# Deeper rings and new planner numbers in a fused attention and two-layer MoE kernel on one core

## The chip, the cores and the metric

The kernel runs on one core of one Trainium2 chip. Five engines work side by side: TensorE (PE in the profile; PEld is its weight load), VectorE (DVE), ScalarE (ACT), GpSimd (POOL) and SyncE (SP), which here issues nearly all DMAs. Each engine runs its own instructions strictly in order and waits for the others by semaphores. The metric is the device time of one execution in microseconds (us). Before the change it is 602.71 us, the median of three runs (602.31, 602.71 and 603.47).

## The reference

```python
kv  = einsum('bhsd,bhse->bhde', k, v)             # 4 batches, 8 heads, 576 rows, 64 columns
out = einsum('bhsd,bhde->bhse', q, kv)            # attention without a softmax
x   = out / sqrt(mean(out**2, -1) + 1e-6) * g_norm        # 2304 rows x 512
h = x @ w_in                                      # 512 -> 2048
x = (h * tanh(softplus(h))) @ w_out               # 2048 -> 512
h = x @ w2_in                                     # 512 -> 1024
e = exp(h - max(h)); s = h * e / (sum(e) + 1e-9)  # per row
x = ((s - mean(s)) / sqrt(var(s) + 1e-6) * g_ln) @ w2_out # 1024 -> 512
```

The four weight matrices arrive as float64; the device sees each number as two 32-bit words and builds float32 from them.

## The kernel before, in words

Every matrix product is made of three fp16 products of split operands (a number is a high fp16 part plus a low one), so ACT writes the high part of an operand and DVE the low part, always in that order.

**Stages.** The 2304 rows are six blocks of 384 rows (three tiles of 128). First come `kv` of each batch (`kv_pair`, L307) and the attention of each block: `a_xo` (L445, PE) writes a tile into a PSUM bank, `a_xc` (L456, ACT) copies it out for blocks 3 to 5 and frees the bank, then square (L461, ACT), row sums (L465, DVE), the power -1/2 (`a_rho`, L470 and L472, POOL), scaling (`a_xf`, L478, DVE), the split (L487 on ACT, L492 on DVE) and a DMA transpose (`a_xT`, L502) into the operand `xT` of the first layer. All late tiles of `xo` and the `kv` products share one bank. Beside it, 48 weight pieces of 512 KB are loaded and decoded: ACT L561, POOL L566, DVE L571 and L578, then the split L589 on ACT and L596 or L598 on DVE.

The first layer works in units of a block and a quarter of the hidden columns. Blocks 0 to 2 use plain products (`h_mm`, L701); blocks 3 to 5 use a seven-product scheme (`h_prod`, L796) on half blocks, for which `conv_x` and `conv_w` (L732, L738, then ACT L744 and DVE L746 into the tile `ws`) make sums of operands. The tile `ws` lies where the attention's tiles lay, so its first write waits for the last attention transpose. The output product of the first layer is `y_mm` (L870).

The second layer takes pairs of row tiles, p = 0 to 8. `y_split` (L918, L920) makes the split operands of pair p in a region given by `y_form`; `emit_H2` (L975) multiplies; ACT L984 and DVE L997 and L1002 put the products together and find the row maximum. Per tile t then follow `s_max` (L1007, DVE), `s_exp` (L1012, ACT), `s_z` (L1018, DVE), `s_sq` (L1023, ACT), `s_den` and `s_rho` (L1029 to L1039, five POOL instructions on one column; L1038 is the power) and `s_ln` (L1045, ACT). The one-column values of a tile lie in a tile `small`, of which four rotate. The normalised rows of the pair are split again: `s_hi` (L1081, ACT) and `s_lo` (L1087, DVE) write a region that `hl` gives, in three parts a, b and c, and `s_T` (L1092) transposes each part by DMA. For p = 0 the region lies in the dead weights `w1` and in `ws`; for all later pairs it is one region in `g`. `emit_O` (L1111) multiplies, ACT L1122 and L1135 and DVE L1130 put the output together.

**What sets the order.** Nothing is written out in issue order. Every step is a `task` with an engine, a cost in us, the tasks that it waits for, and sometimes a due time. `Plan.order` lists the tasks by simulating these costs and always takes, of the tasks that are ready on an engine, the one with the earliest due time; `Plan.search` repeats this 300 times with due times moved at random and keeps the list that ends PE earliest. The instructions are then emitted in that list's order, and this is the order on every engine. Where the list has PE idle early in the kernel, `keep_warm` (L1613) puts in matmuls on the identity matrix whose results nobody reads (called fillers here); their number is fixed by the list. So a changed cost can change the order on all engines, anywhere.

Of the kernel before, what the change touches and what calls it, by code (L numbers as in the profile page):

```python
# [8 lines left out]
FP32 = mybir.dt.float32  # L9
# [133 lines left out]
def tile_attn_moe_moe2(  # L143
# [14 lines left out]
    B, H, S, D = q.shape  # L158
# [6 lines left out]
    NB = NTOK // BLK  # L165
    NU = NB * 4
    G = 4
# [6 lines left out]
    NI = 3  # L174
# [507 lines left out]
    T = {}  # L682
# [218 lines left out]
    def y_form(p):  # L901
        if p not in yF:
            n = p if p < 7 else p - 7
            x = (w1f, w34["ws"])[n % 2][:, 4096 * (n // 2):4096 * (n // 2) + 14 * HB]
            yF[p] = x.rearrange("p (q a c n) -> p q a c n", q=7, a=2, c=2)
        return yF[p]
# [35 lines left out]
    ph2 = {}  # L942
# [12 lines left out]
    def small(t, name):  # L955
        if (t, "small") not in T:
            T[t, "small"] = ph2["p"].tile([128, len(SMALL)], FP32, tag="small", name="small", bufs=4)
        n = SMALL.index(name)
        T[t, name] = T[t, "small"][:, n:n + 1]
        return T[t, name]  # L960
# [89 lines left out]
    def hl(p, x):  # L1050
        lo, hi = T_OF[x]
        if p:
            t = g_h[:, 1024 * lo:1024 * hi]
        elif x == "b":
            t = w34["ws"][:, 0:3072]
        else:
            t = w1f[:, 0:2048] if x == "a" else w1f[:, 2048:4096]
        return t.rearrange("p (q a f) -> p q a f", a=2, f=512)
# [201 lines left out]
    for c in range(4):  # L1260
        u = (0, c)
# [40 lines left out]
    for b, r in tiles:  # L1302
# [12 lines left out]
        task(("rho", *u), "G", 2.0, a_rho, u, [("ms", *u)] + ring("rho", 3, ("xf", *u)))  # L1315
# [168 lines left out]
    for p in range(NP):  # L1484
        where_ = last_H if p == 6 else [("H", NB - 1, p // 2, 0)] if p < 7 else [("T", 0, x) for x in ("ac" if p == 7 else "b")]
# [26 lines left out]
    for p in range(NP):  # L1512
# [27 lines left out]
        for t in (2 * p + 1, 2 * p):  # L1540
            task(("mx", t), "V", 0.15, s_max, (t,),
# [7 lines left out]
            task(("den", t), "G", 0.5, s_den, (t,), [("ex", t)])  # L1549
            task(("pw", t), "G", 1.1, s_rho, (t,), [("sq2", t), ("den", t)])  # L1550
            task(("ln", t), "A", 1.05, s_ln, (t,), [("pw", t)])
    for p in range(NP):
        gone = lambda x: [("T", p - 1, x)] if p > 1 else dead if p else [("2", "ab".index(x) if x in "ab" else 0, 3)]
# [9 lines left out]
        for x, c in (("a", 1.4), ("b", 2.1), ("c", 1.4)):  # L1563
            buf = [("O", p - 2, i) for i in ORDER] if p > 1 else dead if p else [("Yd", NB - 1, 1)]
            task(("T", p, x), "S", c, s_T, (p, x),
                 [("lo", p, x)] + ([("lo", p, "s")] if x == "b" else []) + buf, 2.6)
# [72 lines left out]
    for key, due in ((("xT", 3, 2), 110.0), (("xT", 4, 2), 125.0), (("xT", 5, 2), 135.0)):  # L1639
        plan.tasks[key][5] = due  # L1640
        plan.hints.add(key)
# [46 lines left out]
```

## Time and profile before

| | |
|---|---|
| median of three runs | 602.71 us |
| the profiled execution | 606.54 us |
| its span, first to last instruction | 604.8 us |
| PE busy | 586.6 us, 97% |
| DVE, ACT, POOL busy | 430.1, 370.1, 134.9 us |
| granted TensorE clock, mean | 0.997 |

The profiled execution took 1.74 us more than its span and 3.83 us more than the median of the runs. PE busy includes the fillers, and a matmul that runs at half clock counts as busy too, so 97% hides time. A timeline row reads: start, duration, engine, line, operation, output from inputs, count, and in brackets how long the engine sat idle before it and what ended that. A row of a table by stage reads: stretch and its length, then busy us of each engine with the number of instructions, the granted clock (1.00 is full speed), the DMA engines' busy share and GB/s.

### The profile page before, as it was taken

To read this page: it belongs to the slowest core of one execution; us is meant where nothing else is said; L and a number is where in the kernel's file an instruction comes from. 1 tells how busy PE (TensorE), PEld (TensorE's weight loads), DVE (VectorE), ACT (ScalarE), POOL (GpSimd) and SP (SyncE) were. 2 spreads that over 40 slices of the span, in tenths; PEclk is the share of its full clock that TensorE was granted. 3 is DMA by queue.
4 is the path that set the end of the run, shared out by engine and by line. 5 is a ranking of instruction groups with operands and counts; after the bars stand their busy time and mean duration, and the time that the engine had idled before them with its cause. 6 is when DMAs were issued, how large, how long until landed. Compare 5 with 4: busy or idle time off the path is not lost.

```text
span 604.8 us, 12057 instructions
## 1 busy us (share of the span) xinstructions
PE 586.6 (97%) x4827; PEld 407.1 (67%) x4827; DVE 430.1 (71%) x722; ACT 370.1 (61%) x633; POOL 134.9 (22%) x180
## 2 busy tenths in 40 slices
PE   8899999997999999999999999999999998999997
PEld 6667665664666667777777877775455665666776
DVE  1698679865877688986658867775657686878751
ACT  3677567565665434554648656655867567898661
POOL 1535341116165000000101100000421133335400
PEclk9999999998999999999999999999999999999999
DMA  8998786999654300011423436205061547757595
GB/s 286 302 270 190 206 196 172 269 242 244 129 126 95 103 1 1 19 60 65 155 90 117 156 104 218 97 17 201 1 123 35 122 81 157 163 119 149 118 209 140
DMA packets 134760, 83.89 MB, mean 139 GB/s; under 512 B 100656, under 2 KB 122160, under 8 KB 134704
## 3 DMA queue, kind: packets, MB, share of 16 engines
q1 hardware_dynamic: 134544, 83.12, 55.1%
q8 instruction: 38, 0.62, 0.4%
q14 instruction: 18, 0.15, 0.1%
q10 hardware_dynamic: 160, 0.00, 0.0%
HBM read 46.67 MB, written 12.06 MB: 97 GB/s over the span
## 4 chain that ended last, share of the span: by engine, by line
PE 71%; DMA 10%; ACT 6%; DVE 5%; POOL 3%; issue 2%; SPq 2%; ACTq 0%; POOLq 0%; DVEq 0%
PE y L870 28%; PE hp L796 14%; PE op L1111 10%; PE h L975 9%; PE hp L701 8%; DMA st<-in_moe_w_in_dram 3%; DMA st<-in_moe_w_out_dram 3%; DMA qraw<-in_q_dram 2%; PE kvp L307 1%; DVE st L571 1%; ACT g L1081 1%; DVE P L578 1%; POOL small L1038 1%; DMA w<-g 1%; POOL small L1039 1%
## 5 line engine op out<-in xcount | busy, mean ns | idle before, releaser
L870 PE MATMUL y<-g,w 128*128 128x384 f16 x1152 | 204.1, 328 | 0.3 <-DVE g L852 0.3
L870 PEld LDWEIGHTS <-w 128*128 128x128 f16 x1152 | 111.4, 98 | 68.6 <-issue 2.0
L566 POOL TENSOR_SCALAR st<-st 128x512 f32<-128x512 f32 x48 | 39.3, 823 | 248.5 <-ACT P L561 246.2
L1111 PEld LDWEIGHTS <-w 128*128 128x128 f16 x756 | 73.9, 98 | 16.3 <-issue 3.6
L701 PEld LDWEIGHTS <-w 128*128 128x128 f16 x576 | 55.4, 98 | 38.6 <-issue 1.4
L1111 PE MATMUL op<-yT,w 128*128 128x256 f16 x567 | 72.2, 273 | 3.0 <-ACT g L1122 2.9
L701 PE MATMUL hp<-xT,w 128*128 128x384 f16 x384 | 66.2, 326 | 0.8 <-DMA xT<-xhl 0.8
L796 PEld LDWEIGHTS <-ws 128*128 128x128 f16 x576 | 48.4, 98 | 3.4
L852 DVE SCALAR_TENSOR_TENSOR g<-m,g 128x768 f16<-128x768 f32 x48 | 45.1, 952 | 7.0 <-ACT g L847 6.8
L561 ACT ACTIVATE P<-st 128x512 f32<-128x512 f32 x48 | 32.1, 672 | 22.4 <-DMA st<-in_moe_w_in_dram 11.4
L571 DVE SCALAR_TENSOR_TENSOR st<-st 128x512 int32<-128x512 int32 x48 | 34.1, 723 | 15.5 <-POOL st L566 15.5
L840 ACT ACTIVATE m<-hp 128x384 f32<-128x384 f32 x48 | 23.0, 486 | 31.8 <-PE hp L701 31.6
L847 ACT ACTIVATE g<-m 128x768 f16<-128x768 f32 x48 | 39.5, 837 | 2.0 <-PE y L870 1.5
L796 PEld LDWEIGHTS <-w 128*128 128x128 f16 x432 | 36.6, 98 | 3.2
L975 PE MATMUL h<-st,w 128*128 128x512 f16 x150 | 35.6, 379 | 1.1 <-DVE small L997 1.1
L835 ACT ACTIVATE m<-m 128x384 f32<-128x384 f32 (+1 forms) x24 | 16.3, 681 | 31.9 <-DVE m L822 31.9
L975 PEld LDWEIGHTS <-w 128*128 128x128 f16 x210 | 20.5, 98 | 22.7 <-issue 1.4
L1029 POOL TENSOR_SCALAR small<-small 128x1 f32<-128x1 f32 x18 | 10.3, 570 | 111.4 <-ACT e L1012 111.0
L578 DVE SCALAR_TENSOR_TENSOR P<-P,st 128x512 int32<-128x512 int32 x48 | 33.2, 710 | 0.3
L701 PE MATMUL hp<-yT,w 128*128 128x384 f16 x192 | 33.0, 326 | 0.3 <-DMA yT<-xhl 0.3
L1111 PE MATMUL op<-ws,w 128*128 128x256 f16 x189 | 30.9, 273 | 0.0
L975 PEld LDWEIGHTS <-ws 128*128 128x128 f16 x168 | 16.4, 98 | 20.6 <-issue 2.6
(161 smaller groups left out, 980.4 us busy)
## 6 DMA issues: line engine op xcount, KB each, us to landing
st<-in_moe_w_in_dram SPq DMA_DIRECT2D x24, 512.0 KB, 5.3
st<-in_moe_w_out_dram SPq DMA_DIRECT2D x24, 512.0 KB, 4.7
yT<-in_k_dram SPq DMA_DIRECT2D x16, 288.0 KB, 5.6
yT<-in_v_dram SPq DMA_DIRECT2D x16, 288.0 KB, 6.4
out_dram<-yT SPq DMA_DIRECT2D x18, 256.0 KB, 2.4
w_far<-F SPq DMA_DIRECT2D x15, 256.0 KB, 2.7
w_far<-st SPq DMA_DIRECT2D x11, 256.0 KB, 2.4
yT<-w_far SPq DMA_DIRECT2D x3, 896.0 KB, 4.7
```

Of the source, the lines that this page charges most:

```text
L561: nc.scalar.activation(out=P, in_=v[:, :, 1], func=ACTF.Copy, scale=2.0 ** -111)
L566: nc.gpsimd.tensor_scalar(out=v[:, :, 1], in0=v[:, :, 1], scalar1=0.0, scalar2=1.0, op0=ALU.mult, op1=ALU.mult)
L571: nc.vector.scalar_tensor_tensor(out=v[:, :, 0], in0=v[:, :, 0], scalar=29, in1=v[:, :, 1], op0=ALU.logical_shift_right, op1=ALU.bitwise_or)
L578: nc.vector.scalar_tensor_tensor(out=P.bitcast(I32), in0=P.bitcast(I32), scalar=3, in1=v[:, :, 0], op0=ALU.logical_shift_left, op1=ALU.bit ...
L701: nc.tensor.matmul(out=h_t[b, grp, i], lhsT=w1[:, f, c, wa], rhs=xT_t[b][:, C * xa + c], start=(c == 0 and m == 0), stop=(c == C - 1 and m ...
L796: nc.tensor.matmul(out=p[:, HT * fs:HT * fs + HT], lhsT=lhsT, rhs=x[:, C * xa + 2 * kx + c, HT * n:HT * n + HT], start=(opens and fs == 0 ...
L840: nc.scalar.activation(out=m_t[b, grp, i // 2][:, i % 2], in_=h_t.pop((b, grp, i)), func=ACTF.Mish, scale=2.0 ** -16)
L847: nc.scalar.activation(out=g_t[b, grp][:, 0, 2 * i:2 * i + 2], in_=m_t[b, grp, i], func=ACTF.Copy, scale=64.0)
L852: nc.vector.scalar_tensor_tensor(out=g_t[b, grp][:, 1, j], in0=m_t.pop((b, grp, i)), scalar=64.0, in1=g_t[b, grp][:, 0, j], op0=ALU.mult, ...
L870: nc.tensor.matmul(out=y_t[cc][:, 0:BLK], lhsT=w2[:, grp * G + ii, wa, cc * 128:(cc + 1) * 128], rhs=g_t[b, grp][:, ga, ii], start=(first ...
L975: nc.tensor.matmul(out=T[p, "2" + bank], lhsT=yF[p][:, x, ya, c], rhs=w3[w][:, c, wa], start=(first and m == 0), stop=(m == 5), skip_group ...
L1111: nc.tensor.matmul(out=T[p, bank][:, 0:HB], lhsT=lnTs[p % 2][:, 8 * x + 4 * la + kk], rhs=w4[kk][:, 7 * HB * wa + HB * w:7 * HB * wa + HB ...
```

## The change

Five things change: the ring of `small` tiles goes from four to eight; `hl` gives two regions in turn (even p in `w1` and `ws`, odd p in `g`), and a write waits for the transposes of the pair two before instead of one before; `y_form` puts pairs 7 and 8 elsewhere, after the H2 products of pairs 3 and 4; six planner costs are raised (POOL's `rho`, `den`, `pw`, the maximum, the scaling `ln`, the transpose's lag); and the due times of three late attention transposes move later.

```diff
-            n = p if p < 7 else p - 7
+            n = p if p < 7 else p - 4
...
-            T[t, "small"] = ph2["p"].tile([128, len(SMALL)], FP32, tag="small", name="small", bufs=4)
+            T[t, "small"] = ph2["p"].tile([128, len(SMALL)], FP32, tag="small", name="small", bufs=8)
...
     def hl(p, x):
         lo, hi = T_OF[x]
-        if p:
+        if p % 2:
             t = g_h[:, 1024 * lo:1024 * hi]
...
-        task(("rho", *u), "G", 2.0, a_rho, u, [("ms", *u)] + ring("rho", 3, ("xf", *u)))
+        task(("rho", *u), "G", 2.4 if b >= NI else 2.0, a_rho, u, [("ms", *u)] + ring("rho", 3, ("xf", *u)))
...
-        where_ = last_H if p == 6 else [("H", NB - 1, p // 2, 0)] if p < 7 else [("T", 0, x) for x in ("ac" if p == 7 else "b")]
+        where_ = last_H if p == 6 else [("H", NB - 1, p // 2, 0)] if p < 7 else [("2", p - 4, 3)]
...
-            task(("den", t), "G", 0.5, s_den, (t,), [("ex", t)])
-            task(("pw", t), "G", 1.1, s_rho, (t,), [("sq2", t), ("den", t)])
-            task(("ln", t), "A", 1.05, s_ln, (t,), [("pw", t)])
+            task(("den", t), "G", 1.0, s_den, (t,), [("ex", t)])
+            task(("pw", t), "G", 2.0, s_rho, (t,), [("sq2", t), ("den", t)])
+            task(("ln", t), "A", 1.24, s_ln, (t,), [("pw", t)])
...
-        gone = lambda x: [("T", p - 1, x)] if p > 1 else dead if p else [("2", "ab".index(x) if x in "ab" else 0, 3)]
+        gone = lambda x: [("T", p - 2, x)] if p > 1 else dead if p else [("2", "ab".index(x) if x in "ab" else 0, 3)]
...
-                 [("lo", p, x)] + ([("lo", p, "s")] if x == "b" else []) + buf, 2.6)
+                 [("lo", p, x)] + ([("lo", p, "s")] if x == "b" else []) + buf, 3.3)
...
-    for key, due in ((("xT", 3, 2), 110.0), (("xT", 4, 2), 125.0), (("xT", 5, 2), 135.0)):
+    for key, due in ((("xT", 3, 2), 140.0), (("xT", 4, 2), 160.0), (("xT", 5, 2), 170.0)):
```

The order changes from the first weight pieces to the end. Three places follow.

**ACT, the attention of block 3.** L456 copies a tile of `xo` out of the shared bank, L487 is the split that needs POOL's power, L561 starts the decoding of a weight piece. Before:

```order
L456 ACTIVATE xf<-xo 128x512
L461 ACTIVATE sq<-xf 128x512
L561 ACTIVATE P<-st 128x512 x2
L456 ACTIVATE xf<-xo 128x512
L461 ACTIVATE sq<-xf 128x512
L487 ACTIVATE xhl<-xf 128x512
L890 ACTIVATE yT<-y_1252 128x384
L419 ACTIVATE qhl<-qraw 128x512
L456 ACTIVATE xf<-xo 128x512
```

and now:

```order
L456 ACTIVATE xf<-xo 128x512
L561 ACTIVATE P<-st 128x512
L461 ACTIVATE sq<-xf 128x512
L890 ACTIVATE yT<-y_1652 128x384
L456 ACTIVATE xf<-xo 128x512
L419 ACTIVATE qhl<-qraw 128x512
L461 ACTIVATE sq<-xf 128x512
L890 ACTIVATE yT<-y_1739 128x384
L561 ACTIVATE P<-st 128x512
L419 ACTIVATE qhl<-qraw 128x512
L840 ACTIVATE m<-hp 128x384
L487 ACTIVATE xhl<-xf 128x512
```

The first split L487 has moved behind the second copy by seven rows; the third copy now stands seven rows further on. On PE the second and third `xo` of the block had one group of 12 matmuls of 384 columns between them and now have six.

**ACT, the second layer, from pair 2 to pair 4.** The outputs of L1081 are the regions of `hl`; `w_69` is `w1`. Before, the last write of pair 2 and, three rows on in this list, the first of pair 3 both go to `g`:

```order
L1081 ACTIVATE g<-Q 128x2x512
L1023 ACTIVATE e,small<-w_69,small 128x1024
L1135 ACTIVATE yT<-op 128x256
L1081 ACTIVATE g<-w_69 128x512
L1012 ACTIVATE e,small<-Q,small 128x1024
L984 ACTIVATE P<-h_5582 128x512
L1045 ACTIVATE w_69<-w_69,small 128x1024
```

and now, from the last write of pair 3 (to `g`) to the first of pair 4:

```order
L1081 ACTIVATE g<-w_69 128x2x512
L1023 ACTIVATE e,small<-Q,small 128x1024
L1081 ACTIVATE ws<-Q 128x512
L1122 ACTIVATE g<-op 128x256
L1012 ACTIVATE e,small<-Q,small 128x1024
L1122 ACTIVATE g<-op 128x256
L1045 ACTIVATE Q<-Q,small 128x1024
```

The write that follows a pair's last write to `g` now goes to `ws`, which the pair two earlier used, and waits for that pair's transpose.

**DVE, the last attention tiles and the first conversion.** L492 ends a tile's attention on DVE, L738 and L746 are the sums and the low halves of `ws` for the first seven-product unit, L822 belongs to that unit itself. Before:

```order
L492 TENSOR_TENSOR xhl<-xf,xhl 128x512
L852 SCALAR_TENSOR_TENSOR g<-m,g 128x768
L571 SCALAR_TENSOR_TENSOR st<-st 128x512
L770 TENSOR_TENSOR xs<-st,xs 128x768
L852 SCALAR_TENSOR_TENSOR g<-m,g 128x768
L770 TENSOR_TENSOR xs<-st,xs 128x768
L578 SCALAR_TENSOR_TENSOR P<-P,st 128x512
L732 TENSOR_TENSOR st<-w_69 128x1024 x2
L738 TENSOR_TENSOR st<-st 128x2x256 x4
L746 TENSOR_TENSOR ws<-st,ws 128x1024 x2
```

and now:

```order
L492 TENSOR_TENSOR xhl<-xf,xhl 128x512
L746 TENSOR_TENSOR ws<-st,ws 128x1024 x2
L852 SCALAR_TENSOR_TENSOR g<-m,g 128x768
L894 SCALAR_TENSOR_TENSOR yT<-y_2557,yT 128x384
L732 TENSOR_TENSOR st<-w_69 128x1024 x2
L894 SCALAR_TENSOR_TENSOR yT<-y_2590,yT 128x384
L822 TENSOR_TENSOR m<-hp,st 128x2x192
```

The last attention tile (L492) now stands directly ahead of the low halves of `ws`, and the first L822 five rows behind them; before, two more conversions stood between those halves and the first L822.

## Rows read from the trace of the kernel before

**Rows 1.** Busy time by stage: PE, PEld, DVE, ACT, POOL, clock, DMA.

```profile
140.00:160.00 20.00, 17.26 (x176) 10.61 (x176) 13.09 (x20) 12.66 (x25) 9.16 (x9) 0.91 0.88 187
160.00:480.00 320.00, 320.00 (x2512) 223.43 (x2510) 235.14 (x391) 185.50 (x314) 39.83 (x54) 1.00 0.32 90
480.00:580.00 100.00, 94.05 (x670) 65.30 (x668) 73.47 (x140) 78.19 (x124) 39.12 (x63) 1.00 0.67 136
```

**Rows 2.** Timeline of PE around 140 to 146 us, the rows with idle time.

```profile
140.40 0.83 PE L445 MATMUL xo<-kvr,qT 128*128 128x128 f16 x12 [0.81 <-ACT xf L456]
...
145.52 0.92 PE L307 MATMUL kvp<-yT 96*64 96x64 f32 x24 [2.34 <-ACT xf L456]
```

**Rows 3.** Chain that ended last (start, us, what): the same group of 12, twice.

```profile
146.44 3.73 PE y L870 x12
...
173.29 1.95 PE y L870 x12
```

**Rows 4.** One microsecond by stage: PE busy, clock, DMA.

```profile
147.00:148.00 1.00, 1.00 (x5) 0.50 0.76 103
```

**Rows 5.** Timeline of ACT and DVE around 140 us.

```profile
137.89 0.67 ACT L561 ACTIVATE P<-st 128x512 f32<-128x512 f32 x1 [1.77 <-DMA st<-in_moe_w_out_dram]
...
141.84 1.13 DVE L478 SCALAR_TENSOR_TENSOR xf<-xf,rho 128x512 f32<-128x512 f32 x1 [1.82 <-POOL rho L472]
...
143.00 0.63 ACT L487 ACTIVATE xhl<-xf 128x512 f16<-128x512 f32 x1 [2.00 <-DVE xf L478]
```

**Rows 6.** Timeline of PE from 480 to 580 us, the rows with idle time.

```profile
485.70 1.46 PE L975 MATMUL h<-st,w 128*128 128x512 f16 x6 [1.12 <-DVE small L997]
...
502.56 1.46 PE L975 MATMUL h<-st,ws 128*128 128x512 f16 x6 [1.04 <-ACT P L984]
...
513.69 1.14 PE L1111 MATMUL op<-yT,w 128*128 128x256 f16 x9 [1.54 <-ACT g L1122]
...
558.82 1.46 PE L975 MATMUL h<-st,ws 128*128 128x512 f16 x6 [0.68 <-ACT P L984]
...
576.06 1.14 PE L1111 MATMUL op<-yT,w 128*128 128x256 f16 x9 [1.40 <-ACT g L1122]
```

**Rows 7.** Timeline of DVE and ACT: what these PE waits stood behind.

```profile
484.94 0.69 DVE L997 CUSTOM_DVE_ANT_0 Q<-h,yT 128x512 f32<-128x512 f32 x1 [4.84 <-ACT Q L1045]
...
500.27 0.63 ACT L1081 ACTIVATE g<-w 128x512 f16<-128x512 f32 x1 [3.38 <-DMA w<-g]
...
574.50 1.24 ACT L1045 ACTIVATE Q<-Q,small 128x1024 f32<-128x1024 f32 x1 [2.04 <-POOL small L1039]
```

**Rows 8.** Timeline of POOL's power, twice, and of DVE beside the second.

```profile
443.77 0.55 POOL L1038 TENSOR_TENSOR small<-small,nhalf 128x1 f32<-128x1 f32 x1
...
552.70 3.40 POOL L1038 TENSOR_TENSOR small<-small,nhalf 128x1 f32<-128x1 f32 x1
...
554.47 1.22 DVE L1018 SCALAR_TENSOR_TENSOR Q<-Q,e 128x1024 f32<-128x1024 f32 x1
```

**Rows 9.** Timeline of the longest run of fillers, and DVE at its end.

```profile
45.73 7.37 PE L1613 MATMUL hp<-ident 128*128 128x256 f16 x66
...
52.54 0.74 DVE L598 SCALAR_TENSOR_TENSOR w<-P,gs,w 128x512 f16<-128x512 f32 x1
```

**Rows 10.** Timeline from the last attention product to the first product with `ws`.

```profile
184.22 0.83 PE L445 MATMUL xo<-kvr,qT 128*128 128x128 f16 x12
...
195.22 1.24 SPq L502 DMA_TRANSPOSE yT<-xhl  x1
...
208.99 1.06 ACT L744 ACTIVATE ws<-st 128x1024 f16<-128x1024 f32 x1 [1.95 <-DVE st L738]
...
211.91 1.23 DVE L746 TENSOR_TENSOR ws<-st,ws 128x1024 f16<-128x1024 f32 x1 [0.61 <-ACT ws L744]
...
235.62 1.15 PE L796 MATMUL hp<-xs,ws 128*128 128x192 f16 x12
```

**Rows 11.** The line L502, the attention's transposes: from issue to landing.

```profile
DMA to landing us min/median/max: 3.1/3.4/6.1
```

More of the change, by code (lines that the diff above doesn't have):

```diff
@@ L1540, in tile_attn_moe_moe2 @@
         for t in (2 * p + 1, 2 * p):
-            task(("mx", t), "V", 0.15, s_max, (t,),
+            task(("mx", t), "V", 0.2, s_max, (t,),
                  [("h21", p), ("h22", p)] if t % 2 else [("h11", p), ("h12", p)])
```

## The prediction

> **What bounds the kernel now.** I read the table by stage first, then the timeline of PE for the rows with idle time, then for each of them the engine that it names, back to what that engine stood behind. From 160 to 480 us PE is busy all 320.00 us at full clock [rows 1]: nothing that happens there can be gained, only lost. PE waits in three other places.
>
> The first is 140 to 151 us. PE waits 0.81 and 2.34 us for ACT's copy L456, which frees the shared bank [rows 2]; the group of 12 matmuls behind the second wait takes 3.73 us where it takes 1.95 later [rows 3]. There the granted clock is 0.50, the lower level of 1.2 GHz [rows 4]; what PE had done before was to stand still for 2.34 us. So the place costs 0.81 + 2.34 + (3.73 - 1.95 = 1.78) = 4.93 us. Where ACT was: it waited 1.77 us for a weight piece that had not landed; then its split L487 waited 2.00 us for DVE, which waited 1.82 us for POOL's power, and the copy that PE needed stood behind that split [rows 5], as the order shows. It is a queue in the wrong order, not too much work: ACT is busy 12.66 of 20 us here [rows 1].
>
> The second is the second layer, 480 to 580 us: PE 94.05 of 100 us, DVE 73.47, ACT 78.19 [rows 1]. Five waits carry it: 1.12, 1.04, 1.54, 0.68 and 1.40 us, sum 5.78 [rows 6]. They have three causes. The 1.12 us: DVE's L997, which empties the PSUM bank, waited 4.84 us for ACT's L1045 [rows 7]. L997 also writes the first value of a new `small` tile, and with four of them in turn the new tile takes the place of one whose last reader is that L1045. The 1.04 us: ACT's L1081 waited 3.38 us for the DMA transpose of the pair before, which still read the one region in `g` [rows 7], and the copy L984 that PE needed stood behind it. The other three (1.54 + 0.68 + 1.40 = 3.62 us): ACT stood at L1045, waiting for POOL's last value (2.04 us for the last of the three [rows 7]), with the copy that PE needed behind. POOL's power takes 0.55 us at one time and 3.40 us at another [rows 8].
>
> The third is the start, where the fillers hide the waits. The longest run, 66 matmuls, takes 7.37 us [rows 9].
>
> **The change part by part.** I sum against the profiled execution, 606.54 us, and carry the sum to the median of the runs, 602.71, at the end.
>
> *The ring of eight.* No instruction is added; the tile that L997 takes is now one of eight tiles earlier, whose L1045 ran four pairs before. The wait of 4.84 us goes, and with it PE's 1.12. What is late next for that L997 is its product, which had been ready. Term: -1.12.
>
> *Two regions in turn.* Same instructions, other addresses. The transposes of the pair two before were issued a whole pair of PE work earlier, so the 3.38 us of ACT go and PE's 1.04 with them. The regions for even p are dead weights: in the new order ACT's writes to them wait for a DMA or DVE, and none of the later pairs' for PE. Term: -1.04.
>
> *Pairs 7 and 8 split later.* The splits and sums move from before the H2 product of pair 4 to among pairs 4 and 5. Their eight copies and the DVE work now fall at 480 us and after, where ACT and DVE have some 22 and 27 us free in 100 [rows 1]. Queued behind them are the copies L984 for PE. Between nothing and one wait like those seen (1.54 us [rows 6]); I take 0.5, within the term for new waits.
>
> *POOL's costs.* The planner had 1.1 us for the three instructions behind the square; now 2.0. So it puts more ACT work between the square L1023 and the L1045 of the same tile. Counted in the order, five of the 18 tiles had nothing or a single copy between the two, and one has now; but a chain with a power of 3.40 us in it [rows 8] is not covered by 2.0. At best all 3.62 go, at worst none. I take half, as the new order covers a short chain but not a long one: -1.81.
>
> Here a rule of the Trainium skill bears on the rows. The long power ran from 552.70 to 556.10, and inside that time DVE ran, among others, L1018, a product of two tiles, to 555.69 [rows 8]. The page "SBUF — State Buffer", section "🔬 SBUF: two separate sides", says that GpSimd and VectorE share one pair of ports as an exclusive lock: an instruction of DVE with two SBUF inputs holds it to its end and the other engine is blocked. The trace agrees: the power ends 0.41 us behind that product. By this rule POOL's time is not a cost that can be planned; it depends on which DVE work falls beside it, and a reordered list draws anew. The term would be 0 and the sum below -5.6 instead of -7.4.
>
> *Late attention.* In the new order of PE the second and third attention products of block 3 have six groups of 12 matmuls between them instead of one, 6 x 1.95 = 11.7 us [rows 3], and ACT's third copy has both first splits well ahead of it. The wait of 2.34 us and the half clock behind it should go; between the first and second product only one group is left, so a wait like the 0.81 may stay in part. Term: -(4.93 - 0.5) = -4.43.
>
> *The start.* The list has 14 fillers fewer behind the first products of the first layer. At 7.37 / 66 = 0.112 us each that is 1.6 us if nothing else is late. But at the end of the long run DVE had only just begun the low half of a weight piece that the next products need, at 52.54 against the run's end at 53.10 [rows 9], and DVE's list up to there is nearly the same. Between 0 and -1.6; I take -0.5.
>
> *New waits.* A list that has not run has waits of its own in 60 to 260 us, where the order is new. Bounds: none, and another place like the one at 140 us, 4.93. The nearest row is a single wait of 0.81 [rows 2]; I take two of them, with the half microsecond of pairs 7 and 8 among them: +1.5.
>
> Sum: -1.12 - 1.04 - 1.81 - 4.43 - 0.5 + 1.5 = -7.4 us, or 599.1 for an execution like the profiled one. That one was 3.83 us slower than the median, so some of its long chains are its own; I let the median keep 6/7 of the gain: 602.71 - 6.3 = 596.4 us.
>
> **The rivals.**
>
> *The waits only move* (no gain in the second layer beyond the two rings, a wait like that of 140 us elsewhere). For it: POOL's chains keep their length, as in [rows 8], and the order of all engines is drawn anew. Against it: two of the causes are removed and not moved. Price: 1.12 + 1.04 + 4.43 gained, 4.93 lost again, -1.66, of which 6/7: 601.3. The port rule above leads here.
>
> *All waits go.* -1.12 - 1.04 - 3.62 - 4.93 - 1.6 = -12.3, no new ones, of which 6/7: 592.2. For it: neither ACT nor DVE is full in any stage [rows 1]. Against it: POOL's 3.40 us.
>
> *Slower: the first conversion comes too late.* The tile `ws` may not be written before the last attention transpose, and that tile's product has moved later: in the order only 12 groups of full matmuls and two groups of half size now lie between the last L445 and the first product with `ws`: 12 x 1.95 [rows 3] and twice 1.15 at most [rows 10], some 25 us, where there were 235.62 - 184.22 = 51.4. The chain that must fit: from the product to the transpose's issue 11.0 us (184.22 to 195.22), 3.4 us to land in the median and 6.1 at most [rows 11], and the two ACT and two DVE halves from 208.99 to 213.14, 4.2 us [rows 10]: about 19 us. It fits with 6 us to spare. DVE's list now has these halves five rows ahead of the unit's first sum, so if DVE and ACT run 6 us behind on the attention, PE stops. At 12 us behind it costs 6 us and some 1.8 of half clock behind the stop [rows 3], and the three further conversions follow on DVE at the same distance, each able to add: -7.4 + 7.8 + some 2 more = +2.4, about 605. Below 6 us behind it costs nothing. Nothing in the rows shows such a backlog, but 26 of the 32 us to spare are gone.
>
> *It doesn't do what it says* (the region or ring not the cause): then the two waits of 1.12 and 1.04 stay: -5.2, of which 6/7, 598.2; inside the forecast's own range.
>
> **How the numbers follow.** Forecast, 593 to 600 with 596.4: chance 0.52. Waits only move, 600 to 603: 0.18. All waits go, below 593: 0.15. Slower, above 603: 0.15. A run of this kernel can tell 0.2% (1.2 us) from no change: faster means below 601.5, within means 601.5 to 603.9. Of the second case about half lies below 601.5. So faster 0.52 + 0.15 + 0.08 = 0.75, same 0.11, slower 0.14. The range leaves out the lowest part of the third case and most of the last: 590 to 603.5.
>
> **What would show it.** Ring: no row of L997 waiting for L1045 or POOL by several us. Regions: no L1081 that waits over 1 us for `w<-g`. Late attention: no PE wait on L456 over 1 us between 130 and 200 us, and the clock at 1.00 in every stage up to 480. POOL: L1045's waits for L1039 in 480 to 580 us fewer than before, PE's waits on L1122 and L984 under 2.5 us in sum. Start: the first seven-product group not later than before. Wrong would be: PE idle before the first product with `ws`, a clock of 0.5 anywhere from 60 to 480 us, or PE busy in 480 to 580 us at 94 of 100 again.

## The result and the profile after

The changed kernel takes 596.14 us, the median of four runs (595.62 to 598.38), against 603.09 us for the kernel before beside it (602.31 to 604.91): ratio 0.9888, 95% interval 0.9853 to 0.9922. It is faster by more than the 0.2% that can be told apart. In a later comparison on one chip the same two kernels gave 594.79 against 604.05 us, ratio 0.9839 (0.9815 to 0.9863). So the gain is 7 to 9 us; 596.4 had been forecast.

The profiled execution of the changed kernel took 596.47 us. Its span is 594.7 us where before had 604.8, and its mean clock is 1.000. That difference of 10.1 us is larger than that of the medians, since the profiled execution of before holds the stretch at half clock [rows 4]. Of the 68 executions of before that were timed beside the experiments, 13 have a mean granted clock of 0.997 or less; they took 606.63 us in the mean, and the 55 at 0.999 or 1.000 took 603.59. The median of before, 603.09, is near the second of these.

The table by stage of the changed kernel, with the columns of [rows 1]:

```profile
140.00:160.00 20.00, 19.39 (x191) 12.57 (x190) 10.49 (x17) 10.48 (x20) 5.41 (x6) 1.00 0.84 216
160.00:480.00 320.00, 319.35 (x2575) 222.53 (x2574) 238.23 (x396) 190.13 (x321) 47.88 (x61) 1.00 0.34 91
480.00:580.00 100.00, 98.71 (x746) 72.84 (x745) 76.99 (x144) 78.05 (x124) 35.73 (x58) 1.00 0.79 156
```

In the last row PE is busy 98.71 of the 100 us, where it was busy 94.05, and the granted clock is 1.00 in all three rows. The timeline of the changed kernel's PE has five waits over 0.3 us behind 50 us:

```profile
53.11 1.80 PE L701 MATMUL hp<-xT,w 128*128 128x384 f16 x10 [0.47 <-DVE w L598]
58.82 3.41 PE L701 MATMUL hp<-xT,w 128*128 128x384 f16 x20 [0.72 <-DMA xT<-xhl]
146.91 0.92 PE L307 MATMUL kvp<-yT 96*64 96x64 f32 x24 [0.61 <-DMA yT<-in_v_dram]
177.85 0.92 PE L307 MATMUL kvp<-yT 96*64 96x64 f32 x24 [0.65 <-DMA yT<-in_v_dram]
566.17 1.14 PE L1111 MATMUL op<-yT,w 128*128 128x256 f16 x9 [1.29 <-ACT g L1122]
```

No wait on L456 is left [rows 2], and of the five in the second layer [rows 6] one. The two at 147 and 178 us are new: PE waits there for the loads of `v`, not for ACT.

The 10.1 us are gained as follows. Up to the first layer-1 product of block 1 (start 58.59 before, 58.82 now) nothing is gained. From there to the first H2 product it takes 349.13 instead of 355.72 us: 2.43 us of waits and 1.78 us of half clock are gone, one output group of 12 matmuls (1.95 us) has moved behind that product, and 0.4 us is in no row. From the first H2 product to the end it takes 186.74 instead of 190.46 us, with that group more: 5.94 us of waits have become 1.29, and 1.0 us is in no row.

### The profile page after: what moved, and what is told of

It is laid out like the page before. It is cut to its first block, busy times and chain, and to the rows that moved or that the text cites. A ratio compares the mean times of both kernels' runs of the same rounds, so it can differ in the third digit from the quotient of the medians.

```text
span 594.7 us, 12020 instructions
## 1 busy us (share of the span) xinstructions
PE 583.9 (98%) x4813; PEld 407.4 (69%) x4813; DVE 431.5 (73%) x722; ACT 370.3 (62%) x633; POOL 136.8 (23%) x180
## 4 chain that ended last, share of the span: by engine, by line
PE 86%; DMA 8%; DVE 2%; issue 1%; SPq 1%; ACT 1%; POOL 1%; POOLq 0%; DVEq 0%
PE y L870 30%; PE hp L796 14%; PE h L975 14%; PE hp L701 13%; PE op L1111 13%; DMA st<-in_moe_w_in_dram 3%; DMA yT<-in_v_dram 3%; DMA st<-in_moe_w_out_dram 2%; PE xo L445 1%; PE kvp L307 1%; DMA xT<-xhl 1%; DVE P L578 0%; POOL small L1039 0%; DVE st L571 0%; SPq L262 0%
## 5 line engine op out<-in xcount | busy, mean ns | idle before, releaser
L566 POOL TENSOR_SCALAR st<-st 128x512 f32<-128x512 f32 x48 | 37.4, 785 | 233.7 <-ACT P L561 232.1
L852 DVE SCALAR_TENSOR_TENSOR g<-m,g 128x768 f16<-128x768 f32 x48 | 46.9, 987 | 10.4 <-ACT g L847 10.3
L561 ACT ACTIVATE P<-st 128x512 f32<-128x512 f32 x48 | 32.0, 673 | 26.2 <-DMA st<-in_moe_w_in_dram 13.2
L1029 POOL TENSOR_SCALAR small<-small 128x1 f32<-128x1 f32 x18 | 15.5, 860 | 97.1 <-ACT e L1012 96.6
```

The source lines that it names most:

```text
L561: nc.scalar.activation(out=P, in_=v[:, :, 1], func=ACTF.Copy, scale=2.0 ** -111)
L566: nc.gpsimd.tensor_scalar(out=v[:, :, 1], in0=v[:, :, 1], scalar1=0.0, scalar2=1.0, op0=ALU.mult, op1=ALU.mult)
L852: nc.vector.scalar_tensor_tensor(out=g_t[b, grp][:, 1, j], in0=m_t.pop((b, grp, i)), scalar=64.0, in1=g_t[b, grp][:, 0, j], op0=ALU.mult, ...
```

## The experiments

Each ratio is the one on record, with its 95% interval; it is not always exactly the quotient of the two medians beside it (599.89 / 604.05 is 0.9931, on record is 0.9912). "Second layer" below means PE's waits from 470 us on; the five of [rows 6] sum to 5.78 us before (5.94 with one of 0.16), and after they come to 1.29. The words of an edit such as "the six costs" mean those lines of the diff above, and all else is the kernel before unless said. The list of before is drawn again by nearly every edit; where an edit leaves the list, or a part of it, word for word as it was, I say so, since only there does the edit act alone.

### The ring alone

```diff
-            T[t, "small"] = ph2["p"].tile([128, len(SMALL)], FP32, tag="small", name="small", bufs=4)
+            T[t, "small"] = ph2["p"].tile([128, len(SMALL)], FP32, tag="small", name="small", bufs=8)
```

> The kernel before with eight small tiles instead of four; the list of instructions is the same on every engine, only the addresses of the one-column values differ. Theory of places (each edit carries its own term): DVE's L997 no longer waits for ACT's L1045, PE's 1.12 us at that place goes, 6/7 of it in the median: ratio 0.9984 (0.9978 to 0.999). Theory of the redrawn list (the gain of the change comes from the new order as a whole): a ring alone does nothing, ratio 1.000, since the same L1045 holds the copy that PE needs a moment later.

Measured: 601.81 against 604.58 us, ratio 0.9948 (0.9931 to 0.9965), 2.8 us, more than either theory had. The waits of the second layer that are left, on PE:

```profile
501.45 1.45 PE L975 MATMUL h<-st,ws 128*128 128x512 f16 x6 [0.48 <-ACT P L984]
503.06 2.75 PE L975 MATMUL h<-st,ws 128*128 128x512 f16 x12 [0.16 <-ACT yT L984]
512.58 1.14 PE L1111 MATMUL op<-yT,w 128*128 128x256 f16 x9 [1.54 <-ACT g L1122]
574.09 1.14 PE L1111 MATMUL op<-yT,w 128*128 128x256 f16 x9 [1.39 <-ACT g L1122]
```

With the list unchanged, the 1.12 us went, and with it half of the 1.04 (I had put that down to the region) and the 0.68 us (put down to POOL). DVE's wait of 4.84 us is gone; that its earlier work behind that point is what shortened the other two is argued and not shown.

### Ring and regions

```diff
-            n = p if p < 7 else p - 7
+            n = p if p < 7 else p - 4
...
-        where_ = last_H if p == 6 else [("H", NB - 1, p // 2, 0)] if p < 7 else [("T", 0, x) for x in ("ac" if p == 7 else "b")]
+        where_ = last_H if p == 6 else [("H", NB - 1, p // 2, 0)] if p < 7 else [("2", p - 4, 3)]
...
-            T[t, "small"] = ph2["p"].tile([128, len(SMALL)], FP32, tag="small", name="small", bufs=4)
+            T[t, "small"] = ph2["p"].tile([128, len(SMALL)], FP32, tag="small", name="small", bufs=8)
...
-        if p:
+        if p % 2:
...
-        gone = lambda x: [("T", p - 1, x)] if p > 1 else dead if p else [("2", "ab".index(x) if x in "ab" else 0, 3)]
+        gone = lambda x: [("T", p - 2, x)] if p > 1 else dead if p else [("2", "ab".index(x) if x in "ab" else 0, 3)]
```

> The kernel before with eight small tiles, two regions in turn and pairs 7 and 8 split later; old costs and old due times. The dependences of pairs 7 and 8 reach back through the list, so the order is new everywhere. Theory of places: the waits of 1.12 and 1.04 us go, the ones on POOL stay, and a wait of some us on L456 in the attention of block 3 is there as long as the split L487 stands ahead of the third copy; -1.9 us, ratio 0.997 (0.994 to 0.999). Theory of the redrawn list: a time anywhere between 596 and 606 us, with the attention's wait present or not regardless of the due times.

Measured: 599.09 against 604.58 us, ratio 0.9915 (0.9891 to 0.9938), 5.5 us. Pairs 7 and 8 are split later here too, so "ring and regions" below holds that part as well. The regions can't be run without the ring: with four `small` tiles a step of that list waits for one that stands behind it, and the kernel would never end. The second layer has one wait left:

```profile
571.18 1.14 PE L1111 MATMUL op<-yT,w 128*128 128x256 f16 x9 [1.29 <-ACT g L1122]
```

So ring and regions take PE's waits in the second layer from 5.94 to 1.29 us with the old costs, the one of 1.54 behind POOL [rows 6] among them. Both theories had these stay or move.

### The due times alone

```diff
-    for key, due in ((("xT", 3, 2), 110.0), (("xT", 4, 2), 125.0), (("xT", 5, 2), 135.0)):
+    for key, due in ((("xT", 3, 2), 140.0), (("xT", 4, 2), 160.0), (("xT", 5, 2), 170.0)):
```

> The kernel before with only the three due times moved (140, 160, 170). The list is new up to the first layer's end; in the second layer it is the same as before. The third copy L456 of block 3 still stands right behind the first split L487, and only one group of 12 matmuls lies between the second and third xo. Theory of places, as I had put it: the due times carry the 4.43 us, ratio 0.994 (0.992 to 0.996), and the second layer keeps PE's five waits. Rival: the due times only move the block later as a whole, the split still stands ahead of the copy, so a wait of 1 to 3 us on L456 stays at the new place and the gain is under 2 us, ratio 0.997 to 1.001.

Measured: 604.09 against 604.58 us, ratio 0.9982 (0.9956 to 1.0008): nothing that can be told, as the rival had it. The block comes 20 us later, and its waits with it:

```profile
146.11 0.92 PE L307 MATMUL kvp<-yT 96*64 96x64 f32 x24 [0.75 <-DMA yT<-in_v_dram]
160.50 0.83 PE L445 MATMUL xo<-kvr,qT 128*128 128x128 f16 x12 [0.99 <-ACT xf L456]
168.66 0.92 PE L307 MATMUL kvp<-yT 96*64 96x64 f32 x24 [0.81 <-ACT xf L456]
175.64 0.92 PE L307 MATMUL kvp<-yT 96*64 96x64 f32 x24 [1.11 <-DMA yT<-in_v_dram]
```

3.66 us in four pieces, where before had 3.15 in two [rows 2]. The second layer, whose list is that of before, keeps 5.36 us of its 5.94.

### The six costs alone

```diff
-        task(("rho", *u), "G", 2.0, a_rho, u, [("ms", *u)] + ring("rho", 3, ("xf", *u)))
+        task(("rho", *u), "G", 2.4 if b >= NI else 2.0, a_rho, u, [("ms", *u)] + ring("rho", 3, ("xf", *u)))
...
-            task(("mx", t), "V", 0.15, s_max, (t,),
+            task(("mx", t), "V", 0.2, s_max, (t,),
...
-            task(("den", t), "G", 0.5, s_den, (t,), [("ex", t)])
-            task(("pw", t), "G", 1.1, s_rho, (t,), [("sq2", t), ("den", t)])
-            task(("ln", t), "A", 1.05, s_ln, (t,), [("pw", t)])
+            task(("den", t), "G", 1.0, s_den, (t,), [("ex", t)])
+            task(("pw", t), "G", 2.0, s_rho, (t,), [("sq2", t), ("den", t)])
+            task(("ln", t), "A", 1.24, s_ln, (t,), [("pw", t)])
...
-                 [("lo", p, x)] + ([("lo", p, "s")] if x == "b" else []) + buf, 2.6)
+                 [("lo", p, x)] + ([("lo", p, "s")] if x == "b" else []) + buf, 3.3)
```

> The kernel before with only the six costs raised. The list is new from the first weight pieces to the end. Theory of places: PE's waits behind POOL's power in the second layer (3.62 us) halve, those on the ring and on the region stay, and the attention's wait may stay: -1.55 us in the median, ratio 0.9974 (0.995 to 0.999). Port theory (POOL's long powers come from DVE's instructions beside them and cannot be planned): no gain in 480 to 580 us, ratio 1.000. Redrawn list: the attention of block 3 changes too (its first split now stands behind the second copy by nine rows), and the gain, if any, is there and not in the second layer.

Measured: 595.85 against 604.58 us, ratio 0.9856 (0.9833 to 0.9880), 8.7 us: as much as the whole change, without ring, regions or due times. Neither the places nor the port theory allowed for it, and the theory of the redrawn list had no gain in the second layer, where 5.94 us of waits have become 1.13. All of PE's waits over 0.15 us behind 50 us:

```profile
129.41 0.83 PE L445 MATMUL xo<-kvr,qT 128*128 128x128 f16 x12 [0.68 <-ACT xf L456]
478.53 1.46 PE L975 MATMUL h<-st,w 128*128 128x512 f16 x6 [0.57 <-DVE small L997]
583.62 1.16 PE L1111 MATMUL op<-yT,w 128*128 128x256 f16 x9 [0.56 <-DMA w<-g]
```

In the attention, this list has five groups of 12 matmuls on PE between the third product of block 3 and the `kv` product that needs its copy, where before has one.

### Three of the costs alone

```diff
-            task(("den", t), "G", 0.5, s_den, (t,), [("ex", t)])
-            task(("pw", t), "G", 1.1, s_rho, (t,), [("sq2", t), ("den", t)])
-            task(("ln", t), "A", 1.05, s_ln, (t,), [("pw", t)])
+            task(("den", t), "G", 1.0, s_den, (t,), [("ex", t)])
+            task(("pw", t), "G", 2.0, s_rho, (t,), [("sq2", t), ("den", t)])
+            task(("ln", t), "A", 1.24, s_ln, (t,), [("pw", t)])
```

> The kernel before with three of the six costs raised: den 1.0, pw 2.0, ln 1.24 (POOL's two steps and ACT's scaling in the second layer). The list is the same as before up to the second layer, so the attention keeps its waits of 0.81 and 2.34 us on L456 and the half clock in some executions; only the order of the second layer is new. Theory of the costs (their order covers POOL's chain, and by that also the ring and the region): PE's five waits, 5.78 us, shrink to 1.5 or less in sum, -4 us in the median, ratio 0.9935 (0.991 to 0.996). My prediction's term: half of 3.62, and the ring's 1.12 and the region's 1.04 stay, ratio 0.9974. Port theory: the waits on POOL come back at other tiles, ratio 1.000.

Measured: 602.66 against 603.31 us, ratio 0.9993 (0.9971 to 1.0016): no gain that can be told, though my own term (0.9974) lies within that interval. Only the second layer's list is new here, and the ring's wait on PE has grown:

```profile
483.45 1.46 PE L975 MATMUL h<-st,w 128*128 128x512 f16 x6 [1.99 <-DVE small L997]
500.28 1.46 PE L975 MATMUL h<-st,ws 128*128 128x512 f16 x6 [1.02 <-ACT P L984]
501.90 2.75 PE L975 MATMUL h<-st,ws 128*128 128x512 f16 x12 [0.16 <-ACT yT L984]
511.52 1.14 PE L1111 MATMUL op<-yT,w 128*128 128x256 f16 x9 [1.63 <-ACT g L1122]
```

The waits of 0.68 and 1.40 us at the end are gone, the 1.54 behind POOL is still there (1.63); the sum is 4.80 us. So it isn't the true costs of POOL's steps by themselves that empty the second layer; which of the other three does, with them, was not tried. The clock may hide a part of what these costs gave: five of the 12 executions have a mean clock of 0.998 or less, against two of 29 of before beside them, and the others took 602.2 us in the mean against 603.2. Why the lower clock was more frequent, with the attention's list of before, is open. This run tells one thing more: its attention has the list of before word for word, at a mean clock of 0.999 in the profiled execution, and its waits there are 1.04, 0.20 and 0.55 us, not 0.81 and 2.34. So an execution without the half clock can pay some 1.8 us at that place, and not 4.93; the 3.0 us that the executions of before with the lower mean clock took more fit that (4.93 - 3.0 = 1.9).

### All but the due times

```diff
-    for key, due in ((("xT", 3, 2), 140.0), (("xT", 4, 2), 160.0), (("xT", 5, 2), 170.0)):
+    for key, due in ((("xT", 3, 2), 110.0), (("xT", 4, 2), 125.0), (("xT", 5, 2), 135.0)):
```

(Against the changed kernel.)

> The kernel after with the old due times: costs, ring and regions. Up to the second layer the list is that of the kernel with the six costs alone, with one wait of about 0.7 us in the attention; in the second layer ring and regions are in. Theory of the costs: nothing is left for ring and regions but the two waits of 0.57 and 0.56 us that the costs alone left; ratio 0.9850 (0.983 to 0.988), at or up to 1 us below the costs alone and 1 to 3 us below the full change. My prediction's terms: without the due times 4.43 x 6/7 = 3.8 us of the gain are missing, ratio 0.995.

Measured: 595.80 against 603.31 us, ratio 0.9877 (0.9845 to 0.9909), not to be told from the full change. My terms had 3.8 us of the gain missing here, and they are not missing. The attention has no wait over 0.15 us, the second layer one of 1.28.

### Another seed, no number changed

```diff
-        rng = random.Random(1)
+        rng = random.Random(3)
```

> The kernel before with another seed of the search (3 for 1) and no number changed: the list differs from the first weight pieces to the end of the attention, and is the same behind it. In it the third copy L456 of block 3 stands behind two splits L487 instead of one, with one group of 12 matmuls between second and third xo. Theory of the queue (the split ahead of the copy makes the wait): a wait of 1 to 4 us on L456 as before, ratio 1.000 (0.997 to 1.003). Theory of the redrawn list (any new draw is as likely to gain): the wait is gone or much smaller, ratio 0.993 to 0.997. In both the second layer keeps its 5.8 us.

Measured: 605.96 against 603.31 us, ratio 1.0049 (1.0028 to 1.0071), slower than either theory said. A new draw alone costs 2.7 us here. `Plan.search` moves only the due times of tasks that its list has before 160 us, so the second layer's list is that of before and keeps its waits. The wait on L456 isn't there; two on the loads of `v` are:

```profile
123.37 1.45 PE L307 MATMUL kvp<-yT 96*64 96x64 f32 x24 [2.15 <-DMA yT<-in_v_dram]
153.57 0.92 PE L307 MATMUL kvp<-yT 96*64 96x64 f32 x24 [1.07 <-DMA yT<-in_v_dram]
```

The two splits ahead of the copy, on which I had expected the wait, cost nothing with three groups of PE between the third product and the `kv` product. Behind the first of these waits the clock falls (0.81 in 125 to 130 us), and 11 of the 12 executions have a mean clock of 0.998 or less.

### The six costs with another seed

Beside the six cost lines:

```diff
...
-        rng = random.Random(1)
+        rng = random.Random(2)
```

> The kernel before with the six costs raised and another seed (2 for 1): the second layer's list is that of the six costs with the first seed, the first layer's and the attention's is another draw; there two splits stand ahead of the third copy L456 of block 3, with five groups of 12 matmuls between the second and third xo. Theory of the costs: the second layer's gain of 4 to 5 us is there whatever the draw, ratio 0.985 to 0.992, and the attention costs under 1.5 us more or less than in the first draw. Theory of the redrawn list: the gain of the six costs was one lucky draw; ratio 0.993 to 1.000.

Measured: 601.03 against 603.31 us, ratio 0.9955 (0.9929 to 0.9980). The second layer, whose list the seed leaves as it was, has 0.56 and 0.65 us of waits, so its gain doesn't hang on what is drawn ahead of it. The time does: a wait of 2.54 us for a load of `v` at 26 us with half clock behind it, and in the attention three more:

```profile
128.57 0.83 PE L445 MATMUL xo<-kvr,qT 128*128 128x128 f16 x12 [0.56 <-DVE kvr L324]
132.69 0.83 PE L445 MATMUL xo<-kvr,qT 128*128 128x128 f16 x12 [1.34 <-ACT xf L456]
153.49 0.92 PE L307 MATMUL kvp<-yT 96*64 96x64 f32 x24 [1.79 <-DMA yT<-in_v_dram]
```

With one set of costs, two draws differ by 5 to 6 us (595.85 and 601.03 us; ratios 0.9856 and 0.9955, from two comparisons). Each theory was half right.

### One `kv` product moved by hand

```diff
     order = plan.search(300, 8.0)
+    at_key = {k: n for n, (_, k) in enumerate(order)}
+    a, l, c, y = (at_key[k] for k in (("kv", 3, 0), ("ld", 3, 2), ("kv", 3, 1), ("Y", 1, 1, 2)))
...
+    order[a:c] = [(order[a][0], order[n][1]) if n == y else order[n] for n in range(a + 1, c) if n != l] + [
+        (order[y][0] + 1.0, order[a][1]), (order[l][0] + 1.0, order[l][1])]
```

> The list of before with one move by hand and no new search: the first kv product behind the third late xo (and the load of the batch that waits for it) goes behind the next group of 12 matmuls; all else stands as before. Theory of the queue (PE meets the copy L456 too early): PE's wait of 2.34 us shrinks to 0.4 or less, the stretch at half clock behind it is gone, and the executions with a mean granted clock under 0.999 get rare; median -2 us, ratio 0.9965 (0.994 to 0.998). Rival: the loads of v come later and the next kv products wait for them instead, 1 to 2 us; ratio 0.999 to 1.001. In both the second layer keeps its 5.8 us.

Measured: 607.07 against 604.05 us, ratio 1.0037 (1.0019 to 1.0055): slower, beyond what the rival had. PE in the attention of block 3:

```profile
141.10 0.83 PE L445 MATMUL xo<-kvr,qT 128*128 128x128 f16 x12 [1.23 <-ACT xf L456]
...
146.32 1.62 PE L307 MATMUL kvp<-yT 96*64 96x64 f32 x48 [0.50 <-ACT xf L456]
147.88 2.12 PE L870 MATMUL y<-g,w 128*128 128x384 f16 x12
153.29 1.14 PE L307 MATMUL kvp<-yT 96*64 96x64 f32 x24 [3.29 <-DMA yT<-in_v_dram]
```

The wait on L456 shrank from 2.34 to 0.50 us, as the theory of the queue has it, and 3.29 us came back two `kv` products on. SyncE shows why; the loads of the fourth batch in this kernel:

```profile
147.28 0.33 SPq L262 DMA_DIRECT2D yT<-in_k_dram  x1
147.66 0.46 SPq L262 DMA_DIRECT2D yT<-in_v_dram  x1
```

Two buffers serve these loads in turn, so a load may not be issued before the `kv` product two before it has read its buffer; that one began at 146.32, and the product that needs the load ran at 153.29, 7.0 us later. Before, the same two began at 145.52 [rows 2] and 153.00, 7.5 us apart and without a wait: two groups lay between them, one at half clock (3.73 us [rows 3]), and now a single one. So the place has two limits, the copy and the load, and a move by one group trades one for the other.

### All but the costs

```diff
-        task(("rho", *u), "G", 2.4 if b >= NI else 2.0, a_rho, u, [("ms", *u)] + ring("rho", 3, ("xf", *u)))
+        task(("rho", *u), "G", 2.0, a_rho, u, [("ms", *u)] + ring("rho", 3, ("xf", *u)))
...
-            task(("pw", t), "G", 2.0, s_rho, (t,), [("sq2", t), ("den", t)])
+            task(("pw", t), "G", 1.1, s_rho, (t,), [("sq2", t), ("den", t)])
...
```

(Against the changed kernel; all six lines go back.)

> The kernel after with the six old costs: ring, regions and late due times. Theory of substitutes (ring with regions, or the new costs, either alone empties the second layer's waits): second layer as after, about 1.3 us of waits; the attention's list is another draw, with three groups of 12 matmuls between the third xo and the kv product behind it, so under 2 us of waits there; ratio 0.990 (0.987 to 0.994). My prediction's terms: 1.81 x 6/7 = 1.55 us of the gain are missing, all in 480 to 580 us, where POOL's waits are back at half of 3.62 or more; ratio 0.9915. Theory of the costs as the sole cause: nothing left, 0.997 or above.

Measured: 599.89 against 604.05 us, ratio 0.9912 (0.9886 to 0.9938), the figure of my terms, and not for their reason. The second layer has 1.00 and 0.18 us of waits. The 1.00 stands behind POOL: ACT waits 2.48 us for POOL's last value, and the copy L984 that PE needs comes at the end of the work that ACT then does without a break.

```profile
549.00 1.24 ACT L1045 ACTIVATE Q<-Q,small 128x1024 f32<-128x1024 f32 x1 [2.48 <-POOL small L1039]
...
551.36 0.58 ACT L984 ACTIVATE F<-h 128x512 f32<-128x512 f32 x1
...
551.99 2.75 PE L975 MATMUL h<-P,w 128*128 128x512 f16 x12 [1.00 <-ACT F L984]
```

Yet this is no more than the changed kernel's 1.29. Of the 3.3 us between the two profiled executions, 1.15 lie ahead of the first layer-1 product of block 1, 1.8 between that and the first H2 product (with the group counted that has moved), and 0.4 behind it. The longest waits ahead of the second layer:

```profile
53.62 1.80 PE L701 MATMUL hp<-xT,w 128*128 128x384 f16 x10 [1.49 <-DVE w L598]
59.97 2.27 PE L701 MATMUL hp<-xT,w 128*128 128x384 f16 x13 [0.53 <-DMA xT<-xhl]
169.22 0.83 PE L445 MATMUL xo<-kvr,qT 128*128 128x128 f16 x12 [1.93 <-ACT xf L456]
```

### The changed kernel again, and costs with the ring

The first is the changed kernel itself. The second is the kernel before with the six cost lines and

```diff
-            T[t, "small"] = ph2["p"].tile([128, len(SMALL)], FP32, tag="small", name="small", bufs=4)
+            T[t, "small"] = ph2["p"].tile([128, len(SMALL)], FP32, tag="small", name="small", bufs=8)
```

> The changed kernel once more, beside the candidate below and on one chip with it: ratio 0.9885 to before (0.986 to 0.991).

> The kernel before with the six costs and eight small tiles, and neither regions nor due times: the list is that of the six costs alone, word for word, and only the ring is added. Theory of substitutes: of the two waits of 0.57 us (DVE's L997 behind POOL in the ring) and 0.56 us that the costs alone left, the first goes; ratio 0.985 (0.982 to 0.988), 1 to 2.5 us under the full change. My prediction's terms: ring and costs alone give 1.12 + 1.81 = 2.93, of which 6/7: ratio 0.996, well above the full change.

Measured side by side: the full change 594.79 us, ratio 0.9839 (0.9815 to 0.9863); costs with the ring 595.15 us, ratio 0.9838 (0.9813 to 0.9863). They can't be told apart. Costs with the ring beat the kernel before but not the changed one; the 0.57 us went as expected, and that made no difference that can be told.

## Why the prediction was right, step by step

The median was met, 596.4 us against 596.14, and that was in part luck. My sum was -7.4 us for an execution like the profiled one, and the profiled executions differ by 10.1; the median gained 6.95, so it kept 0.69 of that and not 6/7 (0.86). A sum that was too small and a factor that was too large cancelled, and so did errors among the terms.

*The ring, -1.12.* The mechanism is shown: with the list unchanged the wait goes. The size was off. Alone it gave 2.8 us, as two other waits shrank with it that I had booked elsewhere. Beside the new costs it gives nothing that can be told.

*Two regions, -1.04.* In the changed kernel no L1081 waits for `w<-g`, as put down, and PE's wait of 1.04 us is gone with ring and regions. But half of it goes with the ring alone, and with the costs alone it is gone as well, while all later pairs share one region. What holds is that ring with regions, and the six costs, each empty the second layer (5.94 to 1.29, or to 1.13 us), so they are substitutes; I had added them.

*POOL's costs, -1.81.* The mechanism was right, and the term was wrong as a part of a sum. ACT's waits at L1045 for POOL's last value, for the 14 of 18 tiles that lie in `Q` (in total, how many, the longest), for the kernel before, ring and regions, all but the costs, three of the costs alone, and the changed kernel:

```profile
ACT Q L1045 <- POOL small L1039: 11.6, 8, 2.5
ACT Q L1045 <- POOL small L1039: 8.6, 7, 1.8
ACT Q L1045 <- POOL small L1039: 9.9, 8, 2.5
ACT Q L1045 <- POOL small L1039: 2.5, 2, 2.3
ACT Q L1045 <- POOL small L1039: 2.8, 2, 1.9
```

With the raised costs ACT does other work meanwhile, as put down. With the three alone, PE's waits behind POOL fell from 3.62 to 1.63 us, about the half that I had taken, but the ring's wait grew by 0.87 and the time shows no gain that can be told. With ring and regions and the old costs ACT still waits 8.6 or 9.9 us, and PE hardly notices (1.29 or 1.18 us of waits in all, against 1.29 in the changed kernel). So added to the other two terms this one is worth nothing in the second layer. The costs are worth about 4 us in the full change (0.9912 against 0.9839), but in the start and the attention. There the raised cost of `rho` stands in the attention itself; whether it or the new draw did this was not run apart.

By the line groups, POOL's five instructions per tile take 51.6 us in all before and 56.0 after, so nothing became shorter; only the waits behind them did. The one that is left in the second layer, in the changed kernel, with POOL, DVE and ACT side by side:

```profile
562.17 2.41 POOL L1039 TENSOR_SCALAR small<-small 128x1 f32<-128x1 f32 x1
...
562.17 1.21 DVE L1018 SCALAR_TENSOR_TENSOR Q<-Q,e 128x1024 f32<-128x1024 f32 x1
563.31 0.08 DVE L1018 DVE_READ_ACCUMULATOR Q<-Q,e 128x1 f32 x1
563.31 1.22 DVE L1087 TENSOR_TENSOR g<-Q,g 128x1024 f16<-128x1024 f32 x1
...
564.61 1.24 ACT L1045 ACTIVATE Q<-Q,small 128x1024 f32<-128x1024 f32 x1 [1.93 <-POOL small L1039]
```

A POOL step on one column, 0.26 us in the median, takes 2.41 here, by a profile that is rough on POOL, and ends 0.05 us behind two DVE instructions with two inputs in a row. This fits the exclusive lock on the ports that GpSimd and VectorE share, as the Trainium skill has it (page "SBUF — State Buffer", section "🔬 SBUF: two separate sides"); the trace agrees. Both begin at 562.17, so which of the two was first is not shown. My rival drew from it that the waits would come back at other tiles. They didn't: PE's waits behind POOL fell from 3.62 to 1.29 us while POOL's time rose, as other work covers the chain.

*Late attention, -4.43.* The wait on L456 went, and the clock of the profiled execution stays at 1.00, as put down. But the due times do neither: alone they give nothing, and without them the change loses nothing. And the size was that of one execution: without the half clock the place costs some 1.8 us. At full clock this stage gave about 2 us, not 3.8 (4.43 x 6/7): from block 1 to the first H2 product it takes 349.13 us, where the execution with the list of before at full clock (three of the costs alone) took 353.05, and 1.95 of that difference is the group that only moved. The second layer carried more than I gave it, 4.65 us of waits against 3.97.

*The start, -0.5.* The first product of block 1 comes 0.23 us later, with 14 fillers fewer: of the term's two ends, 0 was the nearer. PE waits 0.47 us for the low half of a weight piece (L598), as [rows 9] had let expect, and 0.72 for a transpose.

*New waits, +1.5.* Two of 0.61 and 0.65 us in the attention make 1.26. That is right in size, but they are not on ACT but on the loads of `v`, and in the second profiled execution of the changed kernel only one, of 0.50, is left. No wait in the second layer is put down to the later split of pairs 7 and 8, for which I had 0.5.

*The rivals.* Slower: no kernel of this study waits at the first product with `ws`, and room and chain were as I had worked them out. In the changed kernel that product starts 26.05 us behind the last attention product (207.12 to 233.17), where I had some 25, and the halves of `ws` are written 18.3 us behind it (at 225.46), where I had about 19. The kernel without the costs comes nearest:

```profile
213.93 0.83 PE L445 MATMUL xo<-kvr,qT 128*128 128x128 f16 x12
...
230.88 1.22 DVE L746 TENSOR_TENSOR ws<-st,ws 128x1024 f16<-128x1024 f32 x1
...
236.08 1.15 PE L796 MATMUL hp<-xs,ws 128*128 128x192 f16 x12
```

There 22.15 us hold a chain of 18.17, and 4 us are to spare. All waits go: no, the median gained 7 to 9 us and not 10.5 (12.3 x 6/7). Waits only move: true of single draws (the other seed), not of the change.

## What to carry to other kernels

When a search draws the order, a changed number acts at the place you changed it for and can act by a new draw elsewhere too: try another seed with no number changed before a gain is put down to a number (here 2.7 us lost without any change, and 5 to 6 us between two draws of the same costs), and look which part of the list the search can move at all. Waits of engines that run one behind the other aren't a list to be added up: undo each part alone and do each alone, and look for those that replace one another. And before a stretch of one profiled execution goes into a sum for the median, see whether the other executions have it.

## What the runs showed of the hardware

Behind a stop of PE the granted clock fell to the lower level in some executions of a kernel and not in others, with the same list. A mean clock of 0.998 or less is taken as its sign; where the stretch lies is seen only in the profiled executions. It was so in 13 of 68 executions of before, 9 of 12 with the moved `kv` product, 11 of 12 with the other seed, one of ten of the changed kernel, and none of 16 of the costs alone, the costs with the ring, and all but the due times; the other edits lie between one of 11 (the ring alone) and 9 of 12 (the costs with another seed). Such an execution of before took 3.0 us more in the mean (606.63 against 603.59). In the profiles, from the first product of the first layer on, a stretch at half clock stands behind stops of 1.91, 2.15, 2.34, 2.48, 2.54 and 3.29 us, and none behind stops of 1.79, 1.93 and 1.99 us. So the price of a stop of some 2 us is not one number, and has to be read from several executions.
